# Key and query blocks of an mLSTM kernel: even heads on the lower partitions, odd heads on the upper

## The chip, the cores and the metric

The kernel runs on one core of a Trainium2 chip. The core has five engines that work side by side: TensorE (PE in the profile; its weight loads are PEld) multiplies matrices and writes to PSUM, VectorE (DVE) does elementwise work and 32x32 block transposes, ScalarE (ACT) does activation functions and copies, GpSimd (POOL) does slower elementwise work, and SyncE (SP) issues the data transfers (DMAs), in this kernel all of them. Each engine works through its own instructions in order and waits on semaphores for the others. The metric is the device time of one execution in microseconds.

## The reference

Two blocks follow each other. The first is an mLSTM cell over 4 batches, 8 heads, 768 steps and a head size of 40:

```python
for t in range(S):
    m_new = np.maximum(f_gate[:, :, t] + m, i_gate[:, :, t])
    f_stab = np.exp(f_gate[:, :, t] + m - m_new)
    i_stab = np.exp(i_gate[:, :, t] - m_new)
    C = f_stab * C + i_stab * outer(v_t, k_t)       # 40x40 per head
    n = f_stab * n + i_stab * k_t
    y_t = sigmoid(o_gate_t) * (C @ q_t) / max(|n . q_t|, 1)
```

Its output, as 3072 rows of 320, goes through a dense layer to 2048 columns, an exact GELU, and a dense layer back to 320 columns. q, k, v and the gates are 4-byte floats. The two weight matrices arrive as 8-byte floats and are converted on the core.

## The kernel before, in words

The 768 steps are cut into 6 chunks of 128 (`NCH`, `L`). Within a chunk the recurrence is done as attention: scores k x q of all pairs of steps, weighted by an exponential of the gates and masked (`W`), times v, plus what the state of earlier chunks gives (`state`, `far`). One chunk of all four batches gives 512 rows for the dense layers.

**Stages.** Two strings of step names, `FRONT` and `DOWN`, fix the order of the work by hand; `play` calls the step functions in that order, and each engine keeps the order in which its instructions were written. `FRONT` runs the cells of chunks 0 and 1, converts the weights (steps K and J, fetched by `fetch`) and runs the dense layers of chunk 0. Then a loop over c = 1 to 5 runs `up` (first dense layer and GELU of chunk c, some 28 us) and `down_steps` (second layer, as seven products of halves) with the cell of chunk c + 1 placed between the products by `DOWN`. There are four such stages with a cell in them, for chunks 2 to 5; the last pass of the loop has none.

**Keys and queries.** The score step needs kT and qT: head dimensions on the partitions, even heads of each pair on partitions 0 to 63 and odd heads on 64 to 127, and the 128 steps of the chunk on the free axis. For chunks 0 and 1 `turn` gets them by TensorE transposes. For chunks 2 to 5 they come from VectorE, which transposes blocks of 32x32. For that the data must lie in the right blocks first: `load_blocks` fetches one batch into a tile `by_block` (the same memory as two of the four q buffers of chunks 0 and 1) or, for the last batch of a chunk, into `blocks3`. k lies on partitions 0 to 63 and q on 64 to 127, with the 8 heads side by side on the free axis. `turn_half` then does two VectorE transposes of 64 partitions for k (one for even, one for odd heads) and two for q (line 471).

**Transfers.** `load_blocks` reads k and q of most batches from copies in DRAM, where a batch's heads and steps form one long axis; `copy_chunk` makes these copies one stage ahead, 2 DMAs of 160 KB a batch (line 159). Then 4 DMAs load a batch (line 168). The first two batches of chunk 2 are read from the inputs themselves, with 16 smaller DMAs each (line 173). SP issues everything in program order, and eight semaphores serve its DMAs in turn, so that one may not be issued before the eighth before it has landed. In a stage with a cell, SP's order around the change is: the block loads of batch 2, which wait for the transposes of batch 1; the copies of a later chunk; the block loads of batch 3 into `blocks3`; the gate values of batch 3 (`g<-M_d`, line 190), which POOL masks (line 422); and kb and vb of batch 3 (line 149), from which POOL makes `vw` (line 510) for the state update (line 605).

**VectorE around the second score step.** The scores of batches 2 and 3 (`scores_two`, line 539, step S2) follow products of the second dense layer on TensorE. On VectorE the order ahead of them is: state sums, k of batch 2, `far` (line 646), q of batch 2, an output sum (line 931), k of batch 3, `far`, q of batch 3.

Of the kernel before, what the change touches and what calls it, by code (L numbers as in the profile page):

```python
# [9 lines left out]
F32 = mybir.dt.float32  # L10
# [6 lines left out]
P = 128  # L17
# [8 lines left out]


FRONT = """
    I2 O0 g0 L0 P0 L1 E k1 t0 P1 P2 k7 w0 N k2 w1 O1 K L2 Q s0 O3 w2 q D k2 d P3 t1 w3 c0 L3 J v0 t2 K K y0 s1 I7 v1
    I8 O2 J g1 L4 I5 c1 K I1 I2 y1 s2 x0 t3 B4 O4 B5 g2 J x1 s3 v2 c2 L5 y2 H T0 x2 G0 v3 g3 c3 K y3 M1 J L6 J A x3  # L30
    M0 K W0 O7 K A O6 O5 J M2 W1 S0 C0 K J J T1 U U K L7 V0 K T2 r J J A G2 K G1 Y0 W2 S1 K M3 C1 A J S2 J K W3 K V1 C2
    Y1 T3 J J U U S3 V2 K K J G3 J Y2 C3 X0 K V3 J K F J F K K B8 F J K F F J K F F F R0 X1 J J K F J F K X2 F J K F
    J Y3 K F R1 J F Z B9 B10 F X3 R2 Z R3 F p"""
DOWN = """
    Z F M1 M0 W0 W1 F L3 Z Z S0 C0 F h0 B3 K2 G1 V0 Q2 M2 W2 G2 F K3 F M3 G0 V1 F W3 Q3 S2 D3 Y0 C2 h2 F Z G3 N F
    Y1 X0 F V2 F V3 X1 Y2 R0 F Y3 R1 j F X2 R2 F X3 R3 F"""
# [3 lines left out]
def kernel(  # L40
# [16 lines left out]
    nc = tc.nc  # L57

    B, H, S, D = q.shape
    L = P  # L60
    NCH = S // L
    NP = H // 2
# [42 lines left out]
    state = [const.tile([P, NP, 2 * D1], F32, name=f"state{b}") for b in range(B)]  # L105
    blocks = const.tile([P, 2, H, DP], F32, name="blocks")
    qb = [blocks[:, n] for n in range(2)] + [const.tile([P, H, DP], F32, name="qb2")]
    by_block = blocks.rearrange("p n h d -> p (n h d)").rearrange("p (h x) -> p h x", h=H)
    kb = [const.tile([P, H, DP], F32, name=f"kb{n}") for n in range(NQ)]
    vb = [const.tile([P, H, D1], F32, name=f"vb{n}") for n in range(NQ)]  # L110
    shared = lambda shape, dt, name: wts.tile(shape, dt, name=name, tag="hi", bufs=5)
# [9 lines left out]
    beyond = gates.tile([P, L], BF16, name="beyond")  # L121
    f_sb = gates.tile([BH, NCH, L], F32, name="f_sb")
    i_sb = gates.tile([BH, NCH, L], F32, name="i_sb")
    kq_d = [[dram.tile([B, H * L, D], F32, name=f"{x}{c}_d") for x in "kq"] for c in range(2, NCH)]
    M_d = dram.tile([NCH - 1, BH, L], F32, name="M_d")
    swapped_d = [dram.tile([P, n, BH], F32, name=f"swapped{n}") for n in (NCH - 2, NCH - 3)]

# [23 lines left out]
            nc.sync.dma_start(out=dst[turn_of(n)][:, :, 0:D] if dst else out_of(n),  # L151
                              in_=src[b, :, c * L:(c + 1) * L, :].rearrange("h p d -> p h d"))

    def copy_chunk(c):

        for b in range(B) if c > 2 else range(2, B):
            for to, src in zip(kq_d[c - 2], (k, q)):
                for x, y in ((src[b, :, c * L:(c + 1) * L, :], to[b]),):
                    nc.sync.dma_start(out=y.rearrange("(h x t) d -> x h (t d)", h=H, x=16),
                                        in_=x.rearrange("h (x t) d -> x h (t d)", x=16))  # L160

    def load_blocks(n, to):

        c, b = divmod(n, B)
        for i, src in enumerate((k, q)):
            for d, w in ((0, 32), (32, D - 32)):
                if n > 2 * B + 1:
                    nc.sync.dma_start(out=to[64 * i + d:64 * i + d + 32].rearrange("t h (g w) -> t (h g) w", w=32)[:, :, 0:w],
                                      in_=kq_d[c - 2][i][b, :, d:d + w].rearrange("(x t) d -> t x d", t=32))
                    continue  # L170
                for g in range(4):
                    t = c * L + 32 * g
                    nc.sync.dma_start(out=to[64 * i + d:64 * i + d + 32, :, 32 * g:32 * g + w],
                                      in_=src[b, :, t:t + 32, d:d + w].rearrange("h t d -> t h d"))

    Mb = {}

# [46 lines left out]
    for j in range(3):  # L224
        m = slice(BH * j, BH * (j + 1))
# [182 lines left out]
    class Cell:  # L408
# [46 lines left out]

        def load_last(self, b):

            self.by_block = fars[0].tile([P, H, P], F32, name="blocks3", tag="x_lo", bufs=1)
            for r in (32, 96):
                nc.gpsimd.memset(self.by_block[r:r + 32], 0.0)  # L460
            load_blocks(self.c * B + b, self.by_block)
# [4 lines left out]
        def turn_half(self, b, i):  # L466
            src = by_block if b < B - 1 else self.by_block
            store, name = ((self.kT, "kT"), (self.qT, "qT"))[i]
            store[b] = two.tile([P, NP, L], F32, name=name, tag=name)
            for hip in range(2):  # L470
                nc.vector.transpose(out=store[b][64 * hip:64 * hip + 64], in_=src[64 * i:64 * i + 64, hip::2])  # L471

        def turn_k(self, b):
            self.turn_half(b, 0)
# [16 lines left out]
        def turn(self, b):  # L491
            n = self.c * B + b
            for src, store, name in ((kb, self.kT, "kT"), (qb, self.qT, "qT")):
                pt = ps_tr.tile([P, NP, L], F32, name="pt", tag="tr")
                unread(pt[:, 0, :])
                for p in range(NP):
                    nc.tensor.transpose(pt[:, p, :], src[turn_of(n)][:, 2 * p:2 * p + 2, :].rearrange("p h d -> p (h d)"),
                                        ident)
                store[b] = two.tile([P, NP, L], F32, name=name, tag=name)
                nc.scalar.copy(out=store[b], in_=pt)  # L500
            if self.c == 1 and b == 1:
                for r in (32, 96):
                    nc.gpsimd.memset(blocks[r:r + 32], 0.0)
                load_blocks(n + 3, by_block)
            if self.c == 1:
                self.weigh_values(b)

# [310 lines left out]
    def up(g, sums_too, turns):  # L818

        def split_to(i):  # L820
            while len(w_lo) <= i:
                split_weight()

        def pair(f, ahead):

            at = [f // 2 * 5 + f % 2 * 3 + x for x in range(NX)]
            split_to(at[1])
            for i in at:
                if i not in w_mid:
                    join_weight(i)  # L830
            pus = [[pool.tile([P, TG], F32, name="pu", tag=tag) for e in range(2)]
                   for pool, tag in (((ps_h, "h"), (ps_mm, "a")), ((ps_tr, "tr"), (ps_mm, "b")))[f % 2]]
            ahead()
            mid = [w_mid.pop(i) for i in at]
            for n, (w, x) in enumerate((([w_hi[i] for i in at], parts["x"]), ([w_lo[i] for i in at], parts["x_lo"]), (mid, parts["x_all"]))):
                for i in range(2):
                    for e in range(2):
                        for k in range(NX):
                            nc.tensor.matmul(pus[i][e], w[k][:, e, i * P:(i + 1) * P], x[:, k, :],  # L839
                                             start=(n == 0 and k == 0), stop=False, skip_group_check=True)  # L840
            return pus

        def rest(u, banks, order):
            mid = w_mid.pop(5 * u + 2)
            for i in order:
                pu = banks[i]
                for n, (w, x) in enumerate(((w_hi[5 * u + 2], parts["x"]), (w_lo[5 * u + 2], parts["x_lo"]), (mid, parts["x_all"]))):
                    for e in range(2):
                        r = halves[e]
                        nc.tensor.matmul(pu[e], w[r, i // 2, i % 2 * P:(i % 2 + 1) * P], x[r, NX, :], start=False,  # L850
                                         stop=(n == 2), skip_group_check=True)

        def out(i, e, pu):
            nc.scalar.activation(out=g.t[:, HF * e + i, :], in_=pu[e], func=AF.Gelu, scale=4097.0)  # L854

        if c == 1:
            copy_chunk(2)
        b0 = pair(0, lambda: split_to(4))
        b1 = pair(1, lambda: join_weight(2))
        for step in turns[:1]:  # L860
            step()
        rest(0, b0 + b1, (0, 1, 2, 3))
        split_to(6)
        join_weight(5)
        join_weight(6)
        for i, pu in enumerate(b0 + b1):
            for e in range(2):
                out(i, e, pu)
        for step in sums_too[:5]:
            step()  # L870
        b2 = pair(2, lambda: split_to(9))
        hidden_sums(g, 0, 2)
        b3 = pair(3, lambda: (hidden_sums(g, 2, 4), join_weight(7)))
        for step in turns[1:] + sums_too[5:]:
            step()
        if c + 2 < NCH:
            copy_chunk(c + 2)
        rest(1, b2 + b3, (2, 3, 0, 1))
        for i, e in ((2, 0), (2, 1), (3, 0), (0, 0), (1, 0), (3, 1), (0, 1), (1, 1)):
            out(4 + i, e, (b2 + b3)[i])  # L880
        hidden_sums(g, HF - 2, HF)
        hidden_sums(g, HF - 4, HF - 2)
# [96 lines left out]
    def in_turn(steps):  # L979
        todo = list(steps)  # L980
        return lambda: todo.pop(0)() if todo else None

    def cell_steps(c, letters, before=None):
# [4 lines left out]
                                  cell.turn_q, cell.weigh_last, cell.read_two,  # L988
                                  cell.last_M, cell.scores_two, cell.load_next, cell.update_two)))

    first_g = Hidden(False)
    n_pieces = range(len(pieces))
    steps = dict(P=fetch, L=lambda n: load(n, 0, 2), O=lambda n: load(n, 2, 4), B=load_M, E=second_gates, N=later_gates,
                 I=keep_clock, k=warm, D=lambda: decays_turned(0, 2, 0, 1), Q=lambda: decays_turned(2, NCH - 1, 1, NCH - 1),
                 d=lambda: decays_last(0, 1), q=lambda: decays_last(1, NCH - 1), r=halves_out, p=halves_back,
                 A=in_turn(first_up_steps(0)), U=in_turn(first_up_steps(1)), F=in_turn(first_down_steps(first_g)),
                 K=in_turn(lambda i=i: conv_one(i) for i in n_pieces), H=products_begin,
                 J=in_turn(lambda i=i: conv_two(i) for i in n_pieces), Z=split_weight)
    steps |= cell_steps(0, "mwgtscvyx") | cell_steps(1, "MWGTSCVYXR")
# [41 lines left out]
```

## Time and profile before

| what | value |
|---|---|
| time, median of 3 runs | 480.49 us (480.19 to 484.45) |
| profiled execution, time | 480.8 us |
| its span | 479.0 us |
| TensorE busy | 468.2 us, 98% |
| VectorE busy | 338.9 us, 71% |
| DMA queue of SP | 48.31 MB in 171712 packets, 48.9% of 16 engines |
| granted TensorE clock | 1.0 throughout |
| VectorE transposes of k and q (line 471) | 64 of 64x512, 45.0 us |

The span is the time from the first to the last instruction in the trace; the execution's own time is a little longer. Busy times are sums over an engine's instructions; the ends of matmuls are modelled, and so a TensorE that is busy 98% can still lose time. A group line of the profile gives the source line, engine, operation, output and inputs with their shapes and the count, then the busy time and the mean of one in ns, then the idle time ahead of it and who ended it. A wait line gives who waited for whom: total us, times, longest us. A timeline line gives start, duration, engine, line, operation and, in brackets, the idle time before it.

### The profile page before, as it was taken

How to read it: one execution, taken by the hardware profiler on the slowest of the kernel's cores; microseconds unless marked ns; L12 is line 12 of the kernel's file. 1: busy time of each engine (PE TensorE's matmuls, PEld its weight loads, DVE VectorE, ACT ScalarE, POOL GpSimd, SP SyncE). 2: the span in 40 equal slices, each digit the busy share in tenths (PEclk: the TensorE clock that was granted, in tenths of full speed). 3: DMA queues.
4: the chain of work that ended last, by engine and by line, in shares of the span. 5: the costliest groups of instructions: out<-in, count | busy, mean ns of one | idle time of the engine just before them, and what ended most of it. 6: DMA issues, size and time to landing. Idle time of an engine off the chain costs nothing.

```text
span 479.0 us, 13005 instructions
## 1 busy us (share of the span) xinstructions
PE 468.2 (98%) x5380; PEld 405.0 (85%) x5380; DVE 338.9 (71%) x726; ACT 244.1 (51%) x521; POOL 78.3 (16%) x120
## 2 busy tenths in 40 slices
PE   7899999999999999999999999999999999999997
PEld 7787888777777989977889977889977899977997
DVE  7899789797879989656588665598665687624321
ACT  6986999844532973202874203874203884211300
POOL 3002210000030232500234500234400212100000
PEclk9999999999999999999999999999999999999999
DMA  9997966279440783930862850772940530100001
GB/s 179 191 221 179 206 163 149 75 197 186 143 84 5 155 157 76 174 63 0 164 148 66 149 95 2 155 156 65 164 83 1 65 67 2 57 2 0 1 1 55
DMA packets 171771, 49.14 MB, mean 103 GB/s; under 512 B 154208, under 2 KB 165248, under 8 KB 171712
## 3 DMA queue, kind: packets, MB, share of 16 engines
q1 hardware_dynamic: 171712, 48.31, 48.9%
q8 instruction: 42, 0.69, 0.6%
q14 instruction: 17, 0.14, 0.1%
HBM read 44.16 MB, written 8.72 MB: 110 GB/s over the span
## 4 chain that ended last, share of the span: by engine, by line
PE 82%; DVE 8%; DMA 5%; SPq 2%; issue 1%; ACT 1%; POOL 0%; DVEq 0%; POOLq 0%
PE po L918 27%; PE pu L839 22%; PE po L895 7%; PE pu L784 6%; PE pu L850 6%; PE ph L638 3%; PE ps L539 2%; DVE qT L471 2%; PE px L678 2%; PE pu L790 2%; DMA g<-M_d 2%; PE pf L594 1%; DVE kT L471 1%; PE ps L523 1%; SPq L151 1%
## 5 line engine op out<-in xcount | busy, mean ns | idle before, releaser
L854 ACT ACTIVATE g<-pu 128x512 f32<-128x512 f32 x80 | 40.8, 614 | 107.7 <-PE pu L850 107.6
L918 PE MATMUL po<-w_out,g 128*128 128x160 f32 x640 | 92.7, 301 | 0.0
L918 PEld LDWEIGHTS po<-w_out,g 128*128 128x128 f32 x640 | 87.8, 190 | 2.3 <-ACT g L854 1.8
L918 PE MATMUL po<-w_sums,sums 128*128 128x160 f32 x320 | 47.0, 303 | 0.0
L918 PEld LDWEIGHTS po<-w_sums,sums 128*128 128x128 f32 x320 | 43.9, 190 | 0.6
L839 PE MATMUL pu<-x_hi,w_in_hi 128*128 128x512 f32 x160 | 41.4, 400 | 0.0
L839 PE MATMUL pu<-x_lo,w_in_lo 128*128 128x512 f32 x160 | 40.6, 396 | 0.0
L448 ACT ACTIVATE W<-W,aT 128x128 f32<-128x128 f32 x128 | 38.7, 388 | 0.4
L839 PEld LDWEIGHTS pu<-x_hi,w_in_hi 128*128 128x128 f32 x160 | 29.4, 188 | 8.2 <-ACT g L854 1.9
L839 PEld LDWEIGHTS pu<-x_lo,w_in_lo 128*128 128x128 f32 x160 | 30.1, 188 | 7.2
L895 PE MATMUL po<-w_out,g 128*128 128x320 f32 x128 | 35.2, 433 | 0.0
L743 DVE TENSOR_TENSOR w_in_mid<-w_in_hi,w_in_lo 128x512 fp32r<-128x512 f32 x20 | 13.8, 688 | 29.5 <-PE pu L839 29.5
L895 PEld LDWEIGHTS po<-w_out,g 128*128 128x128 f32 x128 | 24.0, 190 | 9.6
L771 DVE TENSOR_TENSOR sums<-g 128x512 f32<-128x512 f32 x20 | 13.7, 687 | 25.5 <-ACT g L854 25.5
L839 PE MATMUL pu<-x_all,w_mid 128*128 128x512 f32 x80 | 31.6, 395 | 0.0
L839 PE MATMUL pu<-x_all,w_in_mid 128*128 128x512 f32 x80 | 31.6, 395 | 0.0
L931 DVE TENSOR_TENSOR o_sb<-po,o_sb 128x320 f32<-128x320 f32 (+1 forms) x27 | 12.5, 464 | 25.8 <-PE po L918 21.8
L422 POOL TENSOR_SCALAR_AFFINE_SELECT W<-W 128x1024 f32<-128x1024 f32 (+2 forms) x20 | 21.5, 1078 | 54.6 <-DMA W<-M_d 47.9
L784 PE MATMUL pu<-first_x,w_in 128*128 128x256 f32 x128 | 29.1, 382 | 0.0
L784 PEld LDWEIGHTS pu<-first_x,w_in 128*128 128x128 f32 x128 | 23.8, 190 | 3.5 <-DVE w_in L390 0.4
L667 ACT COPY y_rest<-ob 128x128 f32<-128x128 f32 x16 | 4.8, 298 | 40.7 <-DVE ob L660 38.7
L460 POOL MEMSET blocks<- 32x1024 f32 x8 | 7.6, 945 | 108.5 <-PE pu L850 108.3
(183 smaller groups left out, 910.9 us busy)
## 6 DMA issues: line engine op xcount, KB each, us to landing
W<-M_d SPq DMA_DIRECT2D x16, 512.0 KB, 5.2
bits<-in_moe_w_in_dram SPq DMA_DIRECT2D x20, 256.0 KB, 4.5
bits<-in_moe_w_out_dram SPq DMA_DIRECT2D x16, 320.0 KB, 3.2
ob<-in_o_gate_dram SPq DMA_DIRECT2D x24, 160.0 KB, 3.5
out_dram<-o_sb SPq DMA_DIRECT2D x24, 160.0 KB, 2.0
vb<-in_v_dram SPq DMA_DIRECT2D x14, 160.0 KB, 4.9
kb<-in_k_dram SPq DMA_DIRECT2D x14, 160.0 KB, 4.9
k_d<-in_k_dram SPq DMA_DIRECT2D x14, 160.0 KB, 3.1
```

The costliest lines, as they stand in the source:

```text
L422: nc.gpsimd.affine_select(out=x, in_=x, compare_op=OP.is_ge, fill=1.0e30, base=base, pattern=[[0, H], [1, x.shape[2]]], channel_multiplier=-1)
L448: nc.scalar.activation(out=W[n][:, h, :], in_=src, func=AF.Exp, scale=-1.0, bias=aT[:, self.c, r:r + 1])
L471: nc.vector.transpose(out=store[b][64 * hip:64 * hip + 64], in_=src[64 * i:64 * i + 64, hip::2])
L638: nc.tensor.matmul(ph[r, h, :], Pm[:, h, r], vb[turn_of(n)][:, h, :], start=True, stop=True)
L743: nc.vector.tensor_tensor(out=w_mid[i], in0=w_hi[i], in1=w_lo[i], op=OP.add)
L771: nc.vector.tensor_tensor(out=s1, in0=a21, in1=a22, op=OP.add)
L784: nc.tensor.matmul(banks[-1][e][:, i - i0, :], in_tile(i, x)[:, e, i % 2 * P:(i % 2 + 1) * P], first_x[:, x, t0:t1], start=(x == 0 and i = ...
L839: nc.tensor.matmul(pus[i][e], w[k][:, e, i * P:(i + 1) * P], x[:, k, :], start=(n == 0 and k == 0), stop=False, skip_group_check=True)
L850: nc.tensor.matmul(pu[e], w[r, i // 2, i % 2 * P:(i % 2 + 1) * P], x[r, NX, :], start=False, stop=(n == 2), skip_group_check=True)
L854: nc.scalar.activation(out=g.t[:, HF * e + i, :], in_=pu[e], func=AF.Gelu, scale=4097.0)
L895: nc.tensor.matmul(po[b], g.t[:, f, b * L:(b + 1) * L], w_out[:, f, :], start=(f == 0), stop=(f == NF - 1))
L918: nc.tensor.matmul(bank[at][:, i, :], lhs(j, t), rhs(j), start=(first and i == 0 and j == 0), stop=(i == n - 1 and j == HF - 1), skip_grou ...
```

## The change

The blocks of a batch are laid out anew: partitions 0 to 63 hold the even heads and 64 to 127 the odd heads, and the free axis runs over head pair, then k or q, then the 128 steps. kT of a batch is then one VectorE transpose of 128 partitions and 512 columns, and qT another. The copies in DRAM get the same order, one array for k and q together, split by even and odd heads. A batch is copied by 4 DMAs of 80 KB instead of 2 of 160 KB, and loaded by 4 DMAs of the same sizes as before. The first two batches of chunk 2 now go through DRAM as all others do. The first of them is copied and loaded in a new step `e` near the end of `FRONT`, between R1 and J (the string is otherwise the same, only wrapped anew); the memsets and 16 loads that stood behind the second `turn` of chunk 1 go. The other three batches of chunk 2 are copied at the start of the first `up`, where two were.

```diff
-    kq_d = [[dram.tile([B, H * L, D], F32, name=f"{x}{c}_d") for x in "kq"] for c in range(2, NCH)]
+    kq_d = [dram.tile([B, 2, H * L, D], F32, name=f"kq{c}_d") for c in range(2, NCH)]
-    by_block = blocks.rearrange("p n h d -> p (n h d)").rearrange("p (h x) -> p h x", h=H)
+    by_block = blocks.rearrange("p n h d -> p (n h d)").rearrange("p (m i x) -> p m i x", m=NP, i=2)
-    def copy_chunk(c):
+    def copy_chunk(c, batches=range(B)):
-        for b in range(B) if c > 2 else range(2, B):
-            for to, src in zip(kq_d[c - 2], (k, q)):
-                for x, y in ((src[b, :, c * L:(c + 1) * L, :], to[b]),):
-                    nc.sync.dma_start(out=y.rearrange("(h x t) d -> x h (t d)", h=H, x=16),
-                                        in_=x.rearrange("h (x t) d -> x h (t d)", x=16))
+        for b in batches:
+            for i, src in enumerate((k, q)):
+                for hip in range(2):
+                    nc.sync.dma_start(out=kq_d[c - 2][b, hip].rearrange("(m i x t) d -> i x m (t d)", m=NP, i=2, x=16)[i],
+                                      in_=src[b, hip::2, c * L:(c + 1) * L, :].rearrange("m (x t) d -> x m (t d)", x=16))
     def load_blocks(n, to):
         c, b = divmod(n, B)
-        for i, src in enumerate((k, q)):
+        for hip in range(2):
             for d, w in ((0, 32), (32, D - 32)):
-                if n > 2 * B + 1:
-                    nc.sync.dma_start(out=to[64 * i + d:64 * i + d + 32].rearrange("t h (g w) -> t (h g) w", w=32)[:, :, 0:w],
-                                      in_=kq_d[c - 2][i][b, :, d:d + w].rearrange("(x t) d -> t x d", t=32))
-                    continue
-                for g in range(4):
-                    t = c * L + 32 * g
-                    nc.sync.dma_start(out=to[64 * i + d:64 * i + d + 32, :, 32 * g:32 * g + w],
-                                      in_=src[b, :, t:t + 32, d:d + w].rearrange("h t d -> t h d"))
+                nc.sync.dma_start(out=to[64 * hip + d:64 * hip + d + 32].rearrange("t m i (g w) -> t (m i g) w", w=32)[:, :, 0:w],
+                                  in_=kq_d[c - 2][b, hip, :, d:d + w].rearrange("(x t) d -> t x d", t=32))
...
-            self.by_block = fars[0].tile([P, H, P], F32, name="blocks3", tag="x_lo", bufs=1)
+            self.by_block = fars[0].tile([P, NP, 2, L], F32, name="blocks3", tag="x_lo", bufs=1)
...
-            for hip in range(2):
-                nc.vector.transpose(out=store[b][64 * hip:64 * hip + 64], in_=src[64 * i:64 * i + 64, hip::2])
+            nc.vector.transpose(out=store[b], in_=src[:, :, i, :])
...
-            if self.c == 1 and b == 1:
-                for r in (32, 96):
-                    nc.gpsimd.memset(blocks[r:r + 32], 0.0)
-                load_blocks(n + 3, by_block)
...
         if c == 1:
-            copy_chunk(2)
+            copy_chunk(2, range(1, B))
...
+    def first_blocks():
+        copy_chunk(2, range(1))
+        for r in (32, 96):
+            nc.gpsimd.memset(blocks[r:r + 32], 0.0)
+        load_blocks(2 * B, by_block)
```

More of the change, by code (lines that the diff above doesn't have):

```diff
@@ L28 @@
 FRONT = """
[L29 to L33, printed above, removed]
+    I2 O0 g0 L0 P0 L1 E k1 t0 P1 P2 k7 w0 N k2 w1 O1 K L2 Q s0 O3 w2 q D
+    k2 d P3 t1 w3 c0 L3 J v0 t2 K K y0 s1 I7 v1 I8 O2 J g1 L4 I5 c1 K I1
+    I2 y1 s2 x0 t3 B4 O4 B5 g2 J x1 s3 v2 c2 L5 y2 H T0 x2 G0 v3 g3 c3 K y3
+    M1 J L6 J A x3 M0 K W0 O7 K A O6 O5 J M2 W1 S0 C0 K J J T1 U U
+    K L7 V0 K T2 r J J A G2 K G1 Y0 W2 S1 K M3 C1 A J S2 J K W3 K
+    V1 C2 Y1 T3 J J U U S3 V2 K K J G3 J Y2 C3 X0 K V3 J K F J F
+    K K B8 F J K F F J K F F F R0 X1 J J K F J F K X2 F J
+    K F J Y3 K F R1 e J F Z B9 B10 F X3 R2 Z R3 F p"""
 DOWN = """
@@ L995 @@
                  d=lambda: decays_last(0, 1), q=lambda: decays_last(1, NCH - 1), r=halves_out, p=halves_back,
-                 A=in_turn(first_up_steps(0)), U=in_turn(first_up_steps(1)), F=in_turn(first_down_steps(first_g)),
+                 A=in_turn(first_up_steps(0)), U=in_turn(first_up_steps(1)), e=first_blocks, F=in_turn(first_down_steps(first_g)),
                  K=in_turn(lambda i=i: conv_one(i) for i in n_pieces), H=products_begin,
```

## The prediction

> **What bounds the kernel now.** I read the busy line and the chain of work first, then the waits, then engine timelines of the stages that the change touches. Times are from the profiled execution: span 479.0, 480.8 us in all (1.8 around the span), 0.3 above the median 480.49 of the runs shown.
>
> ```profile
> PE 468.2 (98%) x5380; PEld 405.0 (85%) x5380; DVE 338.9 (71%) x726; ACT 244.1 (51%) x521; POOL 78.3 (16%) x120
> ...
> PE 82%; DVE 8%; DMA 5%; SPq 2%; issue 1%; ACT 1%; POOL 0%; DVEq 0%; POOLq 0%
> ...
> L471 DVE STREAM_TRANSPOSE qT<-blocks 64x512 f32<-64x512 f32 x32 | 22.6, 708 | 0.9
> L471 DVE STREAM_TRANSPOSE kT<-blocks 64x512 f32<-64x512 f32 x32 | 22.4, 701 | 0.3
> ...
> L545 DVE TENSOR_TENSOR W<-ps,W 128x256 f32<-128x256 f32 x24 | 10.0, 417 | 10.1 <-PE ps L539 8.9 <-ACT W L448 1.1
> L545 DVE TENSOR_TENSOR W<-ps,W 64x256 f32<-64x256 f32 x24 | 9.9, 413 | 0.1
> ...
> PEld ps L539 <- DVE qT L471: 2.5, 6, 0.6
> ...
> PE ps L539 <- DVE qT L471: 1.2, 4, 0.3
> ```
>
> Read: TensorE is the bound, so a VectorE saving counts only where TensorE waits for VectorE. The waits name one such place, the second score step of a stage (L539), which waits for the last transpose (L471). Each of the four stages that run a cell, which I call A (158 to 202 us), B (231 to 275), C (304 to 347) and D (376 to 417), has one. The timelines show it in B, TensorE first, then VectorE:
>
> ```profile
> 246.85 2.44 PE L918 MATMUL po<-w_out,g 128*128 128x160 f32 x16
> 249.22 0.78 PE L539 MATMUL ps<-qT,kT 64*64 64x128 f32 x6
> 250.31 1.43 PE L539 MATMUL ps<-qT,kT 64*64 64x128 f32 x56 [0.31 <-DVE qT L471]
> ...
> 252.71 0.61 PE L605 MATMUL pf<-vw,kb 128*40 128x41 f32 x21
> ...
> 242.99 1.42 DVE L471 STREAM_TRANSPOSE kT<-blocks 64x512 f32<-64x512 f32 x2
> 244.44 0.50 DVE L646 TENSOR_TENSOR far<-ph,far 128x328 f32<-128x328 f32 x1
> 244.97 1.45 DVE L471 STREAM_TRANSPOSE qT<-blocks 64x512 f32<-64x512 f32 x2
> 246.43 0.49 DVE L931 TENSOR_TENSOR o_sb<-po,o_sb 128x320 f32<-128x320 f32 x1
> 246.84 1.41 DVE L471 STREAM_TRANSPOSE kT<-blocks 64x512 f32<-64x512 f32 x2
> 248.28 0.50 DVE L646 TENSOR_TENSOR far<-ph,far 128x328 f32<-128x328 f32 x1
> 248.81 1.45 DVE L471 STREAM_TRANSPOSE qT<-blocks 64x512 f32<-64x512 f32 x2
> ```
>
> The bracketed 0.31 understates the stall, since modelled matmul ends cover the rest. I measure it from the start of the product before (L918, 246.85) to the next step (L605, 252.71): 5.86. Without waiting that run needs 2.37 (16 of L918 in the chain) + 1.50 (a score step, the first one of A in the chain) + 0.92 (L594) = 4.79. So B loses 1.07. In the same way A loses 6.60 - 4.79 = 1.81 (174.14 to 180.74), C 1.08 (319.59 to 325.46), and D, which has no L605, 0.32 (390.80 to 395.91). Sum **4.28 us**.
>
> **Part by part.** *Transposes.* 64 of 64x512 become 32 of 128x512. The new form is not in the trace. A row's time does not follow the partitions (L545: 417 ns on 128, 413 on 64) and 128x512 rows of two inputs take 0.69, so I take 0.71; above, it is bounded by both halves one after the other, 1.42. Ahead of the second score step lie four pairs of halves, k and q of the last two batches. In B the new course is: kT 242.99 to 243.70, far to 244.20, qT to 244.91, o_sb to 245.32, kT to 246.04, far not before its product ends (246.11 + 0.81 = 246.92) so to 247.45, qT to 248.2. TensorE comes at 249.22: 1.0 early. C is the same, 1.0 early (320.9 against 321.96). In A the step starts from 171.02 or earlier: qT is done by 175.6 against 176.51. In D only 0.3 is missing and 2.8 is saved. All 4.28 go. What is late next on VectorE is the second far, and it has the 1.0 to spare.
>
> *Copies to DRAM.* Each chunk's 8 copies of 160 KB become 16 of 80 KB, all issued by SP, and before the last batch's block loads, g<-M_d, and the kb and vb loads of that batch.
>
> ```profile
> L159 SPq DMA_DIRECT2D k_d<-in_k_dram x14: 568/598/1132, 133.3 to 306.2; - x14
> ...
> 246.65 0.74 POOL L510 TENSOR_TENSOR vw<-vb,ewT 128x328 f32<-128x328 f32 x1 [1.31 <-DMA vb<-in_v_dram]
> ```
>
> A copy takes SP 0.60, and the next follows 0.643 after it. A half copy is not in the trace: below, 0.30 (the shortest block load, L168), above, 1.13 (the slowest copy). I take 0.643 a copy, because the kb and vb loads of 64 rows (0.63) are not cheaper than those of 128 rows (0.48): 16 copies take 10.3 instead of 5.1. The block loads behind them took 2.8 to 4.5 in a full queue; spread out, I take four at 0.5, 2.0. Block loads of batch 2 now all wait for both transposes, done 1.4 after the first begins, which is when the first of them started before.
>
> So in A: Q done 155.6, loads to 157.6, copies to 167.9, last blocks to 169.9 and landed (3.0) at 172.9. The last kT may start at 176.51 - 0.72 - 0.50 - 0.72 = 174.57: 1.7 spare. g<-M_d lands 175.5 (5.1 after issue), its mask ends 177.3 (1.81), vb lands about then, vw is ready at 178.05 (0.74); L605 of the last batch wants it at 176.51 + 1.50 + 0.92 + 0.37 = 179.3: **1.25 spare**. In B: last blocks landed 244.2 against 247.25, **3.0 spare**; vw 248.85 against 252.0. In C: 316.9 against 320.0, **3.1 spare**; vw 321.6 against 324.75. D copies nothing. With a lag s beyond this, the cost is (s - 1.25) + (s - 3.0) + (s - 3.1), each from zero up. ScalarE's exponentials of that batch start at 178.39 in A behind its own o_sb copy, after the mask.
>
> [...]
>
> *The first two batches.* 16 loads at 62.3 to 72.2 and 16 at 137.05 to 144.8 go. Nothing waits for that SP time: TensorE is busy 52.9 of the 53 us from 40 to 93. In their place step e, behind ob at 117.04: 4 copies to 119.6, SP then waits for the last to land (3.1) at about 122, 4 loads to 124.1. Behind this wait stand two W<-M_d (117.08 before, now about 125.3 done, landed 130.5; masked at 136.24), then an ob load that waits for TensorE until 127.41 anyway: 2.1 spare. Blocks land at 127; used at 135.6. The two memsets (0.94 each) move behind a mask on POOL, which waits from 66.4 to 101. Later 12 copies take 133.28 to 141.0, the 4 loads of batch 1 end by 143 and land by 146 (before: issued until 144.8), used at 154.1. Cost 0; without the 2.1 of cover, the out stores and ewT behind would move by the excess.
>
> Sum: 480.8 - 4.28 = **476.5 us**, 0.9% less. A 1% difference, 4.8 us, is about what a measurement here can tell from none.
>
> **Rivals.** (1) *More than this:* B has a gap of 0.55 inside L605 that the trace gives to no engine ("issue"); if it goes too, and the later runs lie at the median instead of 0.3 above, 475.7 or less. Nothing else on TensorE is left to gain in these stages: without the stalls A and C both last 42.4. Chance 0.16. (2) *The last batch's transfers take part of the place of the transposes in A:* s = 2.75 gives 1.5 back, 478. For it: A's 1.25 is the smallest spare. Against: the lag begins with an emptier queue. Chance 0.10. (3) *The wide transpose costs 1.42:* VectorE gains nothing, the change does not do what it says, 480.9. Against: L545. Chance 0.06. (4) *Slower:* SP's queue becomes the bound between the copies and vw in A, B and C. If a half copy holds SP for over 0.89 us, s passes 3.88 and the cost passes 4.28; at 0.91 the time is 482, over 1% slower from 0.99, and 495 at the slowest row (1.13 and its 0.05 gap). For it: two of 28 copies took about 1.1, and 16 in a row offer more chances. Against: copies land in 2.7 to 4.0 us, well inside the 5.1 that eight issues take, after which SP would have to wait for the first of them. Chance 0.14, of which 0.09 lies beyond 1%.
>
> **Numbers.** The forecast (476 to 477.6) has 0.54. 475.2 to 481.5 leaves out the far end of (1) and most of (4); (3) lies in it, so both ends of the transpose do. Faster by over 1%: (1), 0.16; slower by over 1%: 0.09; the rest 0.75. The likeliest case alone: 475.8 to 477.6.
>
> **What would show it.** Transposes: 32 rows at 0.70 to 0.72, and no L539 wait for L471. From L918 to L605 in B and C 4.8. The half copies: a row near 0.60, and g<-M_d issued 2 to 3 us later than before in A to C. If wrong: L539 waiting for kT behind a DMA, or L605 for vw, means SP (2, 4); a transpose row of 1.4 means (3).

## The result, and the profile after

The changed kernel takes 483.3 us (median; 481.42 to 485.78), the kernel before 480.4 on the same chip: a ratio of 1.0056, with a 95% interval from 1.004 to 1.0073. It is 0.6% slower, where 0.9% faster was forecast. The profiled execution took 482.39 us, its span is 480.6.

The page of the changed kernel, busy times, then one of its DMA queues (packets, MB, share of 16 engines' span), then the chain of work by engine:

```profile
PE 469.9 (98%) x5380; PEld 408.1 (85%) x5380; DVE 313.9 (65%) x694; ACT 244.0 (51%) x521; POOL 77.8 (16%) x120
...
q8 instruction: 42, 0.69, 0.6%
...
PE 84%; DVE 5%; SPq 4%; DMA 3%; issue 1%; ACT 1%; POOL 1%; DVEq 0%; POOLq 0%
```

VectorE has lost 25 us of work, and its share of the chain went from 8% to 5%. SP's own share (SPq), its issuing of DMAs, went from 2% to 4%. The transpose is line 467 now. Its instructions (shortest, median and longest in ns) and what VectorE waited for ahead of them (total us, times):

```profile
L467 DVE STREAM_TRANSPOSE kT<-blocks x16: 700/706/714, 134.8 to 390.3; 128x512 f32<-128x512 f32 x16
L467 DVE STREAM_TRANSPOSE qT<-blocks x16: 669/682/702, 135.4 to 393.2; 128x512 f32<-128x512 f32 x16
its engine sat idle before it (us, times) until:
  DMA blocks<-kq_d: 3.9, 3
```

So 128 partitions cost what 64 did (kT 0.706 against 0.701 us, qT 0.682 against 0.708), and the list of waits has no more entry in which TensorE's second score step (now L531) waits for a transpose. The half copies are as forecast too:

```profile
L162 SPq DMA_DIRECT2D kq_d<-in_k_dram x32: 567/593/1357, 116.1 to 312.9; - x32
```

The transposes and the half copies measure what they were priced at, and the profiled execution is still 6 us above the forecast. Where that comes from shows when the starts of the stages are set beside each other (the first L831 of `up`, L839 before; D ends here at its last sum product, 397.40 against 395.91):

| stretch | forecast, us | after minus before, us |
|---|---|---|
| start to stage A | 0 | -0.77 |
| A | -1.81 | -0.73 |
| B | -1.07 | **+4.09** |
| C | -1.08 | -0.78 |
| D | -0.32 | -0.32 |

B makes the result; A and C gain 1.08 and 0.30 less than forecast. TensorE's timeline in B (start, duration, engine, line, operation; in brackets the idle time ahead):

```profile
247.72 1.57 PE L531 MATMUL ps<-qT,kT 64*64 64x128 f32 x64
249.11 1.09 PE L586 MATMUL pf<-state,qT 64*64 64x41 f32 x64
250.14 0.68 PE L597 MATMUL pf<-vw,kb 128*40 128x41 f32 x21
253.60 0.64 PE L597 MATMUL pf<-vw,kb 128*40 128x41 f32 x11 [2.79 <-issue]
```

The score step now runs without a gap. But after 21 of the 32 products of the state update (L597, L605 before) TensorE stands for 2.79 us. At the same product it had stood for 0.55 before. "Issue" means that the profile knows nothing that TensorE waited for. What follows the stand is slow as well, as the chain of waits in this stretch shows (start, us, what), first of the changed kernel:

```profile
250.21 0.61 PE pf L597 x21
250.81 2.79 issue
253.60 0.64 PE pf L597 x11
254.23 7.21 PE po L910 x32
```

and of the kernel before:

```profile
252.78 0.54 PE pf L605 x21
253.32 0.55 issue
253.87 0.43 PE pf L605 x11
254.30 4.54 PE po L918 x32
```

The same 32 products take 7.21 instead of 4.54 us. The table by stretches of the changed kernel gives the reason (window and length; busy time and instructions of PE, PEld, DVE, ACT and POOL; then the granted TensorE clock, the DMA share and GB/s):

```profile
251.00:252.00 1.00, 0.00 (x0) 0.00 (x0) 0.20 (x1) 1.00 (x5) 0.00 (x0) 1.00 1.20 178
252.00:253.00 1.00, 0.00 (x0) 0.00 (x0) 0.97 (x3) 0.11 (x2) 0.81 (x2) 0.90 0.22 29
253.00:259.00 6.00, 5.40 (x29) 5.32 (x30) 5.76 (x14) 2.16 (x4) 3.29 (x5) 0.50 0.01 3
259.00:260.00 1.00, 1.00 (x7) 1.00 (x6) 0.06 (x1) 0.00 (x0) 0.72 (x1) 0.69 0.00 0
```

The granted clock fell to half from 252.80 to 259.63, for 6.83 us. So B's 5.16 us beyond the forecast are 2.24 of standing (2.79 - 0.55), 2.67 of half clock (7.21 - 4.54), 0.21 in the 11 products between them, also at half clock (0.64 - 0.43), and 0.04 that is left. In A, TensorE waits 0.56 us for `vw`, which is a part of what is missing there.

**What TensorE stands for.** The queue q8 in the first fence holds a kind of transfer that the kernel doesn't issue: 42 packets of 16 KB. TensorE has 5380 products and 5380 weight loads, 10760 instructions, and 42 x 256 is 10752: each packet is taken here as a block of 256 of TensorE's instructions. The 256 are an estimate from these two counts; that the stand lies at a fixed count of instructions, the two kernels with moved borders below show. The packet of this place starts at 251.12, when TensorE has already stopped, and has landed at 252.25; 1.35 us later TensorE goes on. 256 instructions take little time here: from the score step to the stand TensorE needs 2.4 us for them. In the stretch from 248.0 to 252.3, data take all the time of the 16 engines to which the profile counts the block too (packets and MB; then each queue's packets, MB and share of the 16 engines' time):

```profile
DMA packets 2450, 0.90 MB, mean 210 GB/s; under 512 B 2321, under 2 KB 2321, under 8 KB 2449
...
q1 hardware_dynamic: 2449, 0.89, 100.4%
q8 instruction: 1, 0.02, 1.6%
```

In the kernel before, in the 2 us from 250.6 in which its block came, there was nothing else on the queues:

```profile
DMA packets 1, 0.02 MB, mean 8 GB/s; under 512 B 0, under 2 KB 0, under 8 KB 0
```

Most of the 42 blocks cost TensorE nothing that the trace shows: in the kernel before, the list of waits has only two idle times ahead of products that are put down to "issue", 0.77 at 93.68, 1.29 us behind the landing of a 16 KB packet, and the 0.55 at this border. This border costs from 0.38 to 3.11 us in eleven of the twelve kernels.

### The profile page after: what moved, and what is told of

Its sections match the earlier page's. It is cut to its first block, busy times and chain, and to the rows that moved or that the text cites. A ratio compares the mean times of both kernels' runs of the same rounds, so it can differ in the third digit from the quotient of the medians.

```text
span 480.6 us, 12978 instructions
## 1 busy us (share of the span) xinstructions
PE 469.9 (98%) x5380; PEld 408.1 (85%) x5380; DVE 313.9 (65%) x694; ACT 244.0 (51%) x521; POOL 77.8 (16%) x120
## 4 chain that ended last, share of the span: by engine, by line
PE 84%; DVE 5%; SPq 4%; DMA 3%; issue 1%; ACT 1%; POOL 1%; DVEq 0%; POOLq 0%
PE po L910 30%; PE pu L831 21%; PE po L887 7%; PE pu L776 6%; PE pu L842 5%; PE ph L630 3%; PE ps L531 2%; PE px L670 2%; SPq L162 2%; PE pu L782 2%; SPq L154 1%; PE ps L515 1%; DMA g<-M_d 1%; PE pf L586 1%; PE pf L553 1%
## 5 line engine op out<-in xcount | busy, mean ns | idle before, releaser
L910 PE MATMUL po<-w_out,g 128*128 128x160 f32 x640 | 92.7, 302 | 0.0
L910 PEld LDWEIGHTS po<-w_out,g 128*128 128x128 f32 x640 | 87.9, 190 | 2.3 <-ACT g L846 1.8
L910 PE MATMUL po<-w_sums,sums 128*128 128x160 f32 x320 | 49.7, 314 | 0.0
L910 PEld LDWEIGHTS po<-w_sums,sums 128*128 128x128 f32 x320 | 46.6, 199 | 0.6
L831 PE MATMUL pu<-x_hi,w_in_hi 128*128 128x512 f32 x160 | 41.4, 401 | 0.0
L831 PE MATMUL pu<-x_lo,w_in_lo 128*128 128x512 f32 x160 | 40.6, 396 | 0.0
L831 PEld LDWEIGHTS pu<-x_hi,w_in_hi 128*128 128x128 f32 x160 | 29.5, 188 | 8.1 <-ACT g L846 1.9
L831 PEld LDWEIGHTS pu<-x_lo,w_in_lo 128*128 128x128 f32 x160 | 30.1, 188 | 7.1
L831 PE MATMUL pu<-x_all,w_mid 128*128 128x512 f32 x80 | 31.7, 396 | 0.0
L831 PE MATMUL pu<-x_all,w_in_mid 128*128 128x512 f32 x80 | 31.6, 395 | 0.0
L537 DVE TENSOR_TENSOR W<-ps,W 128x256 f32<-128x256 f32 (+1 forms) x48 | 18.1, 415 | 13.8 <-PE ps L531 12.3
```

Of the source, the lines that this page charges most:

```text
L537: nc.vector.tensor_tensor(out=w[r, :, t], in0=ps[i][hip][r, :, t], in1=w[r, :, t], op=OP.mult)
L910: nc.tensor.matmul(bank[at][:, i, :], lhs(j, t), rhs(j), start=(first and i == 0 and j == 0), stop=(i == n - 1 and j == HF - 1), skip_grou ...
```

## The experiments

The theory after the result: 16 DMAs in place of 8 push SP's data loads later, into the moment at which TensorE asks for its next instructions; these come late, TensorE stands, and the clock drops. Rivals: the wide transposes or the new layout are to blame; `vw` comes late because `vb` does; the stand belongs to something that L597 reads. Ratios below are to the kernel before on the same chip, whose medians were 480.58 to 480.63.

### The changed kernel once more

No edit.

> The changed kernel once more, for a second profile. Theory 'page behind data': in the first profile TensorE stood 2.79 us in B inside L597 until a 16 KB block of its own instructions came, whose packet started only when TensorE was already there, and the clock then ran at half for 6.8 us; both together cost some 5 us, the gain of 4 us is eaten. Then this profile shows the same stand at the same instruction, 2 to 3.5 us long, with a stretch of half clock after it, and the time is 481.5 to 485.5. Rival 'chance': the stand belongs to that one execution; then this profile has none, and the lost time lies elsewhere.

Measured: 483.45 us, ratio 1.005 [1.003, 1.007]. The time is as expected, but the long stand is not there: in B TensorE first waits 1.3 us for `vw`, then 0.5 at the same border, and the clock is half for 3.41 us. Over the whole span the list of waits says (total us, times, longest):

```profile
PE pf L597 <- POOL vw L502: 2.7, 3, 1.3
```

So the late data strike in two ways that can stand in for each other: through `vw`, and through the instructions.

### The wide transposes alone

The kernel before with wide transposes on the old layout. Keys and queries of chunks 2 to 5 are mixed up by this, so what it computes for them is not the reference's; the amount of work is the same.

```diff
-            for hip in range(2):
-                nc.vector.transpose(out=store[b][64 * hip:64 * hip + 64], in_=src[64 * i:64 * i + 64, hip::2])
+            nc.vector.transpose(out=store[b], in_=src[:, i::2])
```

> The kernel before with the wide transposes alone: the blocks and the copies stay as they were (8 copies of 160 KB a chunk), and one transpose of 128 partitions takes kT and one qT. Keys and queries are mixed up by this, so the values of chunks 2 to 5 are not the reference's; shapes and work are the same. Theory 'page behind data': the transfers of B are done 2 to 3 us earlier than in the changed kernel, so the instruction block is not held up, the stand in L605 stays under 1.2 us, the clock stays full, and the time is 476.5 to 477.5. Rival 'TensorE is simply there too early': the block comes no sooner after its request, the stand is 2 us or more and the time 479.5 to 482.

Measured: 477.3 us, ratio 0.9928 [0.9906, 0.995]; profiled 476.35. The wide transposes are worth what the forecast gave the whole change (476.5), and the granted clock is 1.0. At the border in B it stands for 0.38 us:

```profile
250.57 0.43 PE L604 MATMUL pf<-vw,kb 128*40 128x41 f32 x11 [0.38 <-issue]
```

### The halves alone

The kernel before, narrow transposes and old layout, with each copy issued as two of 80 KB.

```diff
-                    nc.sync.dma_start(out=y.rearrange("(h x t) d -> x h (t d)", h=H, x=16),
-                                        in_=x.rearrange("h (x t) d -> x h (t d)", x=16))
+                    for h in (slice(0, NP), slice(NP, H)):
+                        nc.sync.dma_start(out=y.rearrange("(h x t) d -> x h (t d)", h=H, x=16)[:, h],
+                                          in_=x.rearrange("h (x t) d -> x h (t d)", x=16)[:, h])
```

> The kernel before with each copy to DRAM issued as two of 80 KB (four heads each), everything else unchanged, transposes narrow. Measures the longer copies by themselves. Theory 'page behind data': TensorE still waits for the narrow transposes in A, B and C, so it comes to L605 later and the lag of 2.5 to 3.5 us in SP's queue is mostly covered; 480.4 to 482.5, at most a short stand in B. Rival 'the halves cost by themselves': over 482.5, with the loss in the copies or in the block loads behind them.

Measured: 486.99 us, ratio 1.0112 [1.0068, 1.0155], above the 480.4 to 482.5 of the theory: that TensorE comes later here did not cover the lag. This is the loss by itself, some 6 us, without any part of the new layout. It has the same signature, at the same product, and 6.83 us of half clock behind it:

```profile
253.32 0.61 PE L606 MATMUL pf<-vw,kb 128*40 128x41 f32 x21
256.69 0.64 PE L606 MATMUL pf<-vw,kb 128*40 128x41 f32 x11 [2.75 <-issue]
```

The two runs add up: 477.3 + 487.0 - 480.6 = 483.7, against 483.3 for the whole change.

### Small DMAs in place of halves

The kernel before with its full copies, and ahead of each chunk's copies 8 DMAs of 2.5 KB into a scratch array that nothing reads. SP issues as many DMAs as with the halves, but hardly more data move.

```diff
+    small_d = dram.tile([8, 16, D], F32, name="small_d")
...
+        for n in range(8):
+            nc.sync.dma_start(out=small_d[n], in_=k[n % B, n // B, 0:16, :])
         for b in range(B) if c > 2 else range(2, B):
```

> The kernel before with 8 small DMAs of 2.5 KB ahead of each chunk's 8 (in chunk 2, 4) copies of 160 KB; they write a scratch array that nothing reads. SP then spends as many issues on a stage as with the halves, but hardly more data is moved. If the loss of the halves comes from the later time at which kb, vb and W follow on SP: g<-M_d issued 3 to 5 us later as in the run with halves, and 484 to 488. If it comes from the halves themselves (more descriptors, smaller pieces in the queue): close to before, 480 to 482.

Measured: 488.14 us, ratio 1.017 [1.0136, 1.0204]. So the later issue does it; the shape of the halves need not. Counted from the starts of A, B and C, g<-M_d goes out 5.5, 6.4 and 5.8 us later than in the kernel before; with the halves it is 5.7, 6.0 and 5.2. The stand is 3.11 us, followed by 3.41 us of half clock. (Its profiled execution, 490.87, also has a clock of 0.53 from 15 to 26 us, where no small DMA has been issued (the first goes out at 137.27); stage A starts some 4 us late there, and that is no effect of the edit.)

### The copies late

The changed kernel, with the next chunk's copies issued behind the last state sum of the cell (a new step `o` after `D3`), when SP's loads for this stage are done.

```diff
-        if c + 2 < NCH:
-            copy_chunk(c + 2)
...
-    ... W3 Q3 S2 D3 Y0 C2 h2 ...
+    ... W3 Q3 S2 D3 o Y0 C2 h2 ...
...
+                      o=lambda: copy_chunk(c + 2) if c + 2 < NCH else None)
```

> The changed kernel with the copies of chunks 3 to 5 moved in SP's order from the end of the first layer to behind the loads of the last batch (after the weighting of the values in the second half of a stage). The g, kb, vb and W loads are then issued some 8 us earlier than in the changed kernel. Theory 'page behind data': these are done before the second score step, but now the copies run during it; they hold the engines busy about half of the time, so the stand is between none and 1.5 us, and the time 476 to 479. If the stand is as long as before (2.5 us or more) with only copies in the queue, any transfer will do. Rival 'TensorE too early': stand 2 us or more, 480 to 483.

Measured: 477.38 us, ratio 0.9933 [0.9907, 0.9959]. Same instructions and halves, another place in SP's order: the loss is gone, and what is left is the gain of the transposes. At the border TensorE stands for 1.12 us, and the clock stays whole:

```profile
251.60 0.43 PE L597 MATMUL pf<-vw,kb 128*40 128x41 f32 x11 [1.12 <-issue]
```

### One 512 KB load late

The changed kernel, copies where it has them, but the load of the next chunk's first gate values (W<-M_d, 512 KB, issued at 246.65 in B) moved behind the load of `ob` in step X0.

```diff
-            if self.c > 1 and b > 0:
+            if self.c > 1 and b > 1:
                 load_M(n + NW)
...
+            if self.c > 1 and b == 0:
+                load_M(n + 1 + NW)
```

> The changed kernel with one 512 KB load (W<-M_d of the next chunk's batch 0) issued after the state update of batch 0's far part (behind X0's ob load) instead of ahead of the kb and vb loads of batch 3. Theory one (TensorE's 16 KB block of instructions waits behind data in stage B): less data is queued when the block is asked for, the stand inside L597 after 21 of its 32 matmuls shrinks from 2.8 us to 1.2 or less, the clock stays full, 477 to 480 us. Rival (vb and with it vw come late because SP issues 16 half copies): one issue of 0.6 us less ahead of vb, the loss falls by 0.6 us in each of A, B and C at most, the clock still falls: 481.5 to 483. Second rival (the block is late for a reason of its own, not for queued data): nothing moves, 483.4.

Measured: 483.4 us, ratio 1.0041 [1.0011, 1.0072]: no gain. This expectation fell, and only half of the theory behind it. The wait for the block did shrink, to 0.57 us, but `vw` took its place. TensorE's timeline in B:

```profile
252.91 0.51 PE L597 MATMUL pf<-vw,kb 128*40 128x41 f32 x16
254.30 0.31 PE L597 MATMUL pf<-vw,kb 128*40 128x41 f32 x5 [0.88 <-POOL vw L502]
255.18 0.43 PE L597 MATMUL pf<-vw,kb 128*40 128x41 f32 x11 [0.57 <-issue]
```

In A it waited 1.86 us for `vw`, against 0.56 in the profiled execution of the changed kernel, and the clock was half for 3.41 us after each of the two. Why g<-M_d, and so `vw`, came later in A (its mask starts at 178.09 against 176.91, the issue was only 0.4 later) stays open. As long as the copies stand ahead of kb and vb, taking one load away exchanges one late arrival for the other.

### Both late

The changed kernel with the two edits above together.

> The changed kernel with both moves: the copies behind D3 and the 512 KB W<-M_d behind X0's ob load. Theory one (instruction block behind data): the 1.3 us gap that was left in B with the copies late falls under 0.8, time 476 to 477.2, below the 477.4 of the copies late alone. Rival (the rest of that gap is not from queued data): 477.4, no change.

Measured: 476.45 us, ratio 0.9916 [0.9899, 0.9933], which beats both kernels; profiled 476.29. The clock is 1.0, and the stand is down to that of the kernel before:

```profile
250.66 0.43 PE L597 MATMUL pf<-vw,kb 128*40 128x41 f32 x11 [0.57 <-issue]
```

Stage by stage it gains -1.84 (A), -1.06 (B), -1.06 (C) and -0.31 (D), 4.27 in all.

### The border moved by 24 instructions

The changed kernel with 6 more idle products at the start (`warm(6)` to `warm(12)`, where TensorE stood idle for 1.47 us in the kernel before). With borders at fixed counts of instructions from the program's start, each now falls 24 instructions, 12 products, earlier in the work.

```diff
     gates_turned((a[:, 0:1], aT[:, 0:1]))
-    warm(6)
+    warm(12)
```

> The changed kernel with 6 more of the idle products that keep TensorE busy at about 4 to 7 us (24 more instructions of TensorE, 12 matmuls in the trace). The borders between TensorE's 256-instruction blocks then fall 24 instructions earlier in the program. Theory (the stand in B is TensorE waiting for its next block of instructions): the stand moves with the border, from after 21 to after 9 of the 32 matmuls of L597, and is about as long (2 to 3 us); time 482 to 485. Rival (the stand belongs to what L597 reads, or to an engine that the profile does not name): it stays after 21 of 32.

Measured: 479.78 us, ratio 0.9987 [0.9966, 1.0008]. The place is as expected: after 9 products instead of 21, with the operands of L597 untouched.

```profile
252.01 0.38 PE L597 MATMUL pf<-vw,kb 128*40 128x41 f32 x9
252.97 0.66 PE L597 MATMUL pf<-vw,kb 128*40 128x41 f32 x23 [0.58 <-issue]
```

The size is not: 0.58 us instead of 2 to 3. A wait of 1.38 us for `vw` in A made TensorE come to B later, and its block started only 0.22 us after it had passed the border before, although the queues were still full of data (86%); why it was let in so soon stays open. The clock stayed whole. So one and the same program of transfers costs 483.3 or 479.8 us, depending on where 6 idle products let the borders fall.

### The border moved the other way

The changed kernel without some of the idle products of the first 30 us. The step names ask for 11 less; the 3 of `I8` change nothing, because `I5` sets the number anew before it is used. The trace has 5364 products and as many weight loads, against 5380: 32 instructions less and not 44, so the border falls 16 products later and not 22.

```diff
-    ... P1 P2 k7 w0 ... k2 d P3 ... s1 I7 v1 ... I8 O2 J ...
+    ... P1 P2 k3 w0 ... k1 d P3 ... s1 I4 v1 ... I5 O2 J ...
```

> The changed kernel with 11 of the idle products of the first 30 us left out (44 instructions of TensorE, 22 matmuls in the trace; nothing else reads them). The border between blocks then lies 22 matmuls later in the program: after 11 of the L910 matmuls that follow L597 in B instead of after 21 of L597. One such matmul takes 0.15 us, so TensorE reaches the border about 1.6 us later. Theory (the stand is the block asked for at the border before, and landing too late): no stand in L597, at most 1.4 us in L910, the clock stays full, 478 to 480.5 us. Rival (the stand is not tied to the border): a stand of 2 us or more after 21 of L597 and half clock after it, 482 to 485.

Measured: 482.03 us, ratio 1.0022 [0.9992, 1.0052], above what was expected. In B the stand moved out of L597 and into the products after it: behind 5 of them, which is 16 products later, as it must be for 32 instructions. From one product to the next it is 0.98 us, and the clock stays whole there:

```profile
258.00 0.95 PE L910 MATMUL po<-w_sums,sums 128*128 128x160 f32 x5
259.63 3.66 PE L910 MATMUL po<-w_sums,sums 128*128 128x160 f32 x25 [0.68 <-issue]
```

But the list of waits shows new stands in A (total us, times, longest):

```profile
PE pf L597 <- POOL vw L502: 2.9, 3, 1.7
PE po L910 <- issue: 1.8, 2, 1.1
PE pf L586 <- issue: 1.2, 1, 1.2
```

The L586 one and one of L910 lie in A, each 1.6 us behind the landing of a 16 KB packet: the shift moved A's borders too, and A has half clock for 3.41 us. I had priced the shift for B alone. The profiled execution, 485.07, was the slowest of ten (from 478.75), so it shows more of these stands than the median has.

### Both late, and the border moved

The kernel with both transfers late and the same change of the step names, again 32 instructions less.

> The kernel with the copies and the 512 KB W<-M_d both late, and the same 11 idle products left out. Its remaining 0.57 us gap in L597 in B should go: by the theory 475.7 to 476.2 us against 476.45; if fewer idle products cost time at the start (TensorE's clock), or the next border opens a gap of its own, 476.4 or more.

Measured: 475.1 us, ratio 0.9874 [0.9851, 0.9898], the fastest of all, and 0.6 below what was expected. All 32 products of L597 run through:

```profile
251.57 0.81 PE L597 MATMUL pf<-vw,kb 128*40 128x41 f32 x32
252.31 4.84 PE L910 MATMUL po<-w_sums,sums 128*128 128x160 f32 x32
```

B gains 1.64 us on the kernel before, its 1.07 of stalls and the 0.55 stand. The profiled execution took 477.8: in it the clock was half for 10.24 us from about 14 us on (as in the one with the small DMAs, which has all idle products), and stage A starts 1.38 us later than before. So it does not show where the rest of the 1.35 us between the medians of this kernel and of the one with both late comes from.

### The block of B in all twelve kernels

Start and landing of the 16 KB packet are from the trace's records of transfers. "Passes" is when TensorE, counted in products and weight loads, is 256 instructions ahead of the border; "goes on" is its first instruction behind the border. The share of the data is the time of the data packets that start between passing and the packet's start, in parts of the 16 engines' time; as their whole time is counted, it can exceed 100%. A number of instructions in a name is by how much the program's start is longer or shorter.

| kernel | passes | packet starts | wait | data on the queues meanwhile | lands | goes on | landing to going on |
|---|---|---|---|---|---|---|---|
| before | 250.64 | 251.35 | 0.71 | 0 | 252.50 | 253.87 | 1.38 |
| wide alone | 247.66 | 248.35 | 0.69 | 0 | 249.28 | 250.57 | 1.29 |
| both late | 247.56 | 248.36 | 0.80 | 58% | 249.29 | 250.66 | 1.37 |
| both late, -32 | 249.99 | 250.94 | 0.96 | 68% | 251.87 | 253.21 | 1.34 |
| copies late | 247.95 | 249.20 | 1.25 | 60% | 250.13 | 251.60 | 1.47 |
| changed, again | 250.31 | 252.00 | 1.68 | 136% | 253.43 | 254.86 | 1.43 |
| W late | 250.99 | 252.74 | 1.74 | 124% | 253.87 | 255.17 | 1.31 |
| -32 instructions | 254.87 | 257.21 | 2.34 | 80% | 258.14 | 259.62 | 1.48 |
| changed | 248.22 | 251.12 | 2.90 | 100% | 252.25 | 253.60 | 1.35 |
| halves alone | 251.26 | 254.26 | 3.01 | 92% | 255.41 | 256.69 | 1.27 |
| small DMAs | 255.35 | 258.52 | 3.17 | 102% | 259.83 | 261.15 | 1.32 |
| +24 instructions | 249.87 | 250.09 | 0.22 | 86% | 251.47 | 252.97 | 1.50 |

In every kernel TensorE goes on 1.27 to 1.50 us after its block has landed, whatever the data did. The packet never starts before TensorE has passed the place 256 instructions ahead. The wait from there to the packet's start is 0.7 us with empty queues, 0.8 to 1.25 with queues at 58 to 68%, and 1.7 to 3.2 with queues at 80% and more; the three longest are the kernels with the long stand. The last row is the exception told above. The border is the same count of TensorE's instructions in all twelve. In the kernel "both late, -32" TensorE hardly waits there: 0.25 us from one product to the next. That the block is asked for at that place is inferred from these starts; no record shows the request.

## Why the prediction was wrong

- **Transposes: right.** 0.71 us forecast, 0.706 and 0.682 measured. The four stalls were sized right: 1.81, 1.07, 1.08 and 0.32 forecast, 1.84, 1.06, 1.06 and 0.31 gained where the copies and W are late. The sum, 4.28, was right to 0.01 there.
- **Cost of a half copy: right.** 0.643 from one to the next was assumed, the row is 0.593 with 0.05 behind it.
- **SP's lag: too small.** The four block loads behind the copies were taken at 2.0 us together; they hold SP for 3.81 in A, 3.75 in B and 3.39 in C. g<-M_d was to go out 2 to 3 us later than before; counted from the starts of the stages it went out 4.7, 6.3 and 4.4 later. `vw` was done at 179.53, 250.45 and 327.52; with the stages' own starts that is an s of 2.25, 3.1 and 3.3, which the rule prices at 1.0, 0.1 and 0.2, where no cost was forecast. Measured, A is 1.08 short: L597 takes 1.50 us to the next product instead of 0.75, because of `vw`, and in L586 TensorE pauses 0.34 from one product to the next, 1.5 us behind the landing of another 16 KB packet. C is 0.30 short, with 0.25 between two products of L597, for `vw`.
- **The step that failed: "With a lag s beyond this, the cost is (s - 1.25) + (s - 3.0) + (s - 3.1), each from zero up."** It charged a late SP only with what the second score step and L597 read. In B that makes 0.1 us, and in the profiled execution it was indeed no operand that stopped B. But g<-M_d and all behind it were issued 4.8 us later (243.33 against 238.51), and that moved 0.9 MB of data, 100.4% of the 16 engines' time, into the 4.3 us in which TensorE's block was wanted. That cost 2.24 us of standing, and 2.67 + 0.21 more because the clock was halved, which the working took as 1.0 throughout. With all stretches the account closes: 476.5 + 5.16 (B) + 1.08 (A) + 0.30 (C) - 0.77 (start) + 0.13 (behind D) = 482.40, and the profiled execution took 482.39.
- **Rivals.** (4), the slower side, named SP's lag and was right in kind; its price was wrong. It needed a half copy of over 0.89 us, and 0.593 was enough. (1) did not come, but it named the place: the 0.55 gap that "the trace gives to no engine" was the mark of this very border. I counted it as something that might go; it was the thing to ask what makes it longer. (2) happened in part (the late `vw` in A), beside the larger loss in B. (3) was out.
- **The first two batches: cost about nothing, as forecast.** Stage A starts 0.77 us earlier after the change and 0.33 earlier with both late; the kernel with the old front and wide transposes starts it 0.37 earlier, so this is the size of the scatter.

What stays open: why `vw` came later still in A with W late, and what the instruction packet waits for when data are on the queues: in all kernels of the table but the one with 24 instructions more it starts later then, and no record shows why.

## What to carry to other kernels

A gap that the trace puts down to "issue" in the middle of a run of short products may be an instruction block that is late: look for the 16 KB packet beside it (in the twelve kernels it had landed 1.27 to 1.50 us before TensorE went on), and ask what will be on the queues when it is wanted. A transfer that nobody waits for soon was not free to issue here: with 8 DMAs of 2.5 KB ahead of each chunk's copies the kernel before took 488.14 us instead of 480.58. What helped was to put it behind the loads of the stage, where it filled the queues to 58 to 68% when the block was wanted, and not ahead of them, so that they filled the queues (100% in the changed kernel) just when 256 instructions last 2.4 us. And price a stand of TensorE with the half clock that may follow it: behind the stand of 2.79 us it lasted 6.83 us and about doubled the loss (2.24 and 2.67).

## What the runs showed of the hardware

**Instruction blocks.** At this border, where the 256 instructions last only 2.4 us, a block that finds the queues empty is not in time either: 0.7 to wait, 0.93 to 1.14 to carry and 1.3 to 1.4 until TensorE goes on (the first two rows of the table) make 2.9 to 3.2, and so the kernel before stood 0.55 us here, and the one with the wide transposes alone 0.38. With the borders 24 instructions earlier the stand in B moved from behind product 21 of L597 to behind product 9, with 32 later to behind product 5 of L910.

**The clock after an idle time.** Idle time of TensorE in one place, and the half clock behind it:

| kernel, stage | idle, us | half clock, us |
|---|---|---|
| copies late, B | 1.12 | none |
| +24 instructions, A | 1.38 | none |
| -32, B | 0.60 and 0.68 | none |
| W late, B | 0.88 and 0.57 | 3.41 |
| changed, again, B | 1.26 and 0.46 | 3.41 |
| -32, A | 1.19 and 1.68 | 3.41 |
| W late, A | 1.86 | 3.41 |
| halves alone, B | 2.75 | 6.83 |
| changed, B | 2.79 | 6.83 |
| small DMAs, B | 3.11 | 3.41 |

The half clock lasted 3.41 us in five of these rows and 6.83, twice that, in two. An idle time of 1.86 us, or two of 0.88 and 0.57, had it behind them; one of 1.38, or two of 0.60 and 0.68, had not. What sets whether the half clock comes, and whether it is one such length or two, no run here shows.
